# Local attention heads on 64-row tiles: two heads side by side instead of zero halves

## The chip, the cores and the metric

The kernel runs on one core of a Trainium2 chip. The metric is the device time of one execution in microseconds (us), as the median of several runs. The engines are TensorE (PE, with its weight loads as PEld), VectorE (DVE), ScalarE (ACT), GpSimd (POOL) and SyncE (SP), which issues most of the DMAs.

## The reference

Sparse attention (4 batches, 8 heads, 576 positions, head size 64, all fp32) is followed by a top-1 mixture of experts (2304 tokens of width 512, 8 experts, hidden width 1024). Heads 0 to 3 are local: a query sees itself and the 31 positions before it. Heads 4 to 7 are strided: a query sees the earlier positions that leave the same remainder by 32.

```python
mask_local = (rel >= 0) & (rel < stride)                     # heads 0..3, stride = 32
mask_strided = (rel >= 0) & (pos[None] % stride == pos[:, None] % stride)
attn = softmax(where(mask, q @ k.T / 8, -1e9)); x = attn @ v  # then [2304, 512]
expert = argmax(x @ w_gate);  out = gate * relu(x @ w1[expert]) @ w2[expert]
```

## The kernel before, in words

Attention comes first and the experts follow. The attention part is a hand-written software pipeline of 25 steps (line 24, `SEQ`): 16 strided units (`z`) and 9 local units (`l`). A unit passes through five stages: A transposes queries and keys on TensorE and copies them out of PSUM, B makes scores with a mask matmul and narrow matmuls, takes the row maximum and subtracts it (both on DVE), then ACT takes the exponential, C transposes the probabilities, D multiplies with the values and divides by the sum, and E stores the result and transposes it for the gate. In each iteration of the loop that starts at line 928 every engine gets C of unit i, A of i+3, B of i+2, E of i-1 and D of i, in this order. `gating` (line 894) adds gate matmuls (`l_f`), and `drip_out` adds small routing work, most of it on DVE.

A local unit `vv` holds 256 tokens in blocks of 32 queries. Each block needs 64 keys: its own 32 and the 32 before. Two heads (a pair) stand one above the other on the 128 partitions, head 0 on partitions 0 to 63. `K0L` (line 174) is a key tile with a column range for each head, and the half that belongs to the other head is zero; one matmul of 128 rows and 128 columns thus gives the scores of both heads (line 493). `V0L` (line 175) does the same for the values with 130 columns (line 529). The zeros are written by POOL at the start (lines 196 to 207). Each of these fp32 matmuls shows as two instructions in the trace, so the 16 matmuls of a stage show as 32.

`load_l` (line 252) loads the queries and keys of a pair with one DMA each, in runs of 1536 B. `l_r` (line 454) then reorders half of such a tile so that the two heads stand side by side, keys on ACT and queries on DVE, and `l_a` (line 462) transposes the reordered tile on TensorE (line 471) and copies it out: queries on ACT (line 473), keys of head 0 on ACT and of head 1 on DVE (line 477). There are 8 pairs with two halves each, so `l_a` runs 16 times. `load_lv` (line 260) loads the values: a small DMA from POOL (line 266) and, for each head, one DMA from SP of 64 partitions x 17 blocks x 256 B (line 269), which reads nearly each value twice, since a block's row holds the block to its left as well. Values of pairs 4 to 7 reuse the four tiles and so wait for stage D of earlier units.

Loads are put on SP's queue by a planner (`load_more`, line 851) in the order in which they fall due; behind one another stand the strided keys and queries (`load_z`, line 235), strided values (`load_zv`, line 247), `load_l` and `load_lv`. ACT's queue issues the stores of x. Score tiles of both kinds share one PSUM pool, `ps_s`, with two buffers (line 145). The expert part (from line 1089) is dense fp32r matmuls and starts when the first expert is known.

Of the kernel before, what the change touches and what calls it, by code (L numbers as in the profile page):

```python
# [29 lines left out]
RB = 2  # L30
RE = "sv"
ZSTR = "001 3cd23"
ZS = {int(a[0]): a[1:] for a in ZSTR.split()}
TY = 2
# [7 lines left out]
VE = "gg"  # L42
VL = 2
NBS = "-1 0 1 2"
NB = dict(zip(("zq", "zv", "lq", "lv"), map(int, NBS.split())))
ND = 0
RJ = 0
RL = 2
LS = 1
RM = 1  # L50
# [18 lines left out]
def kernel(  # L69
# [68 lines left out]
    with ExitStack() as p1:  # L138
# [6 lines left out]
        ps_s = p1.enter_context(tc.tile_pool(name="ps_s", bufs=2, space=PSUM))  # L145
# [28 lines left out]
        K0L = [cp.tile([128, 2, 608], F32, name=f"k0l{i}") for i in range(4)]  # L174
        V0L = [cp.tile([128, 2, 18, 65], F32, name=f"v0l{i}") for i in range(4)]
# [20 lines left out]
        def zeros_k(i):  # L196
            nc.gpsimd.memset(K0L[i][0:64, 1], 0.0)
            nc.gpsimd.memset(K0L[i][64:128, 0], 0.0)
            for h in range(2):
                nc.gpsimd.memset(K0L[i][64 * h:64 * h + 64, h, 0:32], 0.0)  # L200

        def zeros_v(i):
            nc.gpsimd.memset(V0L[i][0:64, 1], 0.0)
            nc.gpsimd.memset(V0L[i][64:128, 0], 0.0)
            for h in range(2):
                nc.gpsimd.memset(V0L[i][64 * h:64 * h + 64, h, :, 64], 1.0)
                nc.gpsimd.memset(V0L[i][64 * h:64 * h + 32, h, 0, 0:64], 0.0)

        zeros_k(0)
        zeros_k(1)  # L210
# [41 lines left out]
        def load_l(c):  # L252
            b, pair = divmod(c, 2)
            h0 = 2 * pair
            for src, dst, nm in ((k, lk, "lk"), (q, lq, "lq")):
                t = ld.tile([96, 2, 6, 64], F32, tag=nm, name=nm)
                nc.sync.dma_start(out=t, in_=src[b, h0:h0 + 2].rearrange("h (p g) d -> p h g d", g=6))
                dst[c] = t

        def load_lv(c):  # L260
            b, pair = divmod(c, 2)
            h0 = 2 * pair
            vt = V0L[c % 4]
            if c >= ND:
                for h in range(2):
                    nc.gpsimd.dma_start(out=vt[64 * h + 32:64 * h + 64, h, 0, 0:64], in_=v[b, h0 + h, 0:32, :])  # L266

                    src = bass.AP(tensor=v.tensor, offset=v[b, h0 + h, 0:1, 0:1].offset, ap=[[D, 64], [32 * D, 17], [1, D]])
                    nc.sync.dma_start(out=vt[64 * h:64 * h + 64, h, 1:18, 0:64], in_=src)
                return  # L270
            for h in range(2):
                nc.sync.dma_start(out=vt[64 * h + 32:64 * h + 64, h, :, 0:64], in_=v[b, h0 + h].rearrange("(k p) d -> p k d", p=32))

        def copy_lv(c):

            vt = V0L[c % 4]
            for h in range(2):
                {"s": nc.scalar.copy, "v": nc.vector.tensor_copy, "g": nc.gpsimd.tensor_copy}[VE[h]](
                    vt[64 * h:64 * h + 32, h, 1:18, 0:64], vt[64 * h + 32:64 * h + 64, h, 0:17, 0:64])
# [96 lines left out]
        def z_b(u):  # L376
            K0 = K0S[u % 2]
            qt = qts.pop(u)
            s = ps_s.tile([128, 4, 2, 36], F32, tag="s", name="sz")
# [72 lines left out]
        lr = {}  # L452

        def l_r(i):

            c, gi = divmod(i, 2)
            for src, nm in ((lk[c], "k"), (lq[c], "q")):
                t = ld.tile([96, 3, 2, 64], F32, tag="r" + nm, name="r" + nm, bufs=RB)
                {"g": nc.gpsimd.tensor_copy, "v": nc.vector.tensor_copy, "s": nc.scalar.copy}[RE[nm == "q"]](t.rearrange("p g h d -> p h g d"), src[:, :, 3 * gi:3 * gi + 3, :])
                lr[i, nm] = t  # L460

        def l_a(c, gi):
            for nm in "kq":
                src = lr.pop((2 * c + gi, nm))
# [5 lines left out]
                for i in range(3):  # L470
                    nc.tensor.transpose(t[:, i, :], src[:, i].rearrange("p h d -> p (h d)"), ident[:96, :96])
                if nm == "q":
                    nc.scalar.copy(QTL[c % 4].rearrange("d (p g) -> d g p", g=6)[:, 3 * gi:3 * gi + 3, :], t)
                else:
                    for h in range(2):
                        r = slice(64 * h, 64 * h + 64)
                        (nc.vector.tensor_copy if h else nc.scalar.copy)(
                            K0L[c % 4][r, h, 32:32 + S].rearrange("d (p g) -> d g p", g=6)[:, 3 * gi:3 * gi + 3, :],
                            t[r],
                        )  # L480

        MSEL = {0: 0, 2: 4, 4: 2, 6: 4}

        def l_b(vv):
            s = ps_s.tile([128, 2, 2, 128], F32, tag="s", name="sl")
            a = {0: 0, 2: 5, 4: 2, 6: 4}.get(vv, 1)
            nc.tensor.matmul(s, lhsT=identb, rhs=bc(ml[:, a:a + 2], 2, 4), start=True, stop=False, skip_group_check=True)
            for t in range(2):
                for pair in range(2):
                    for c in range(4):  # L490
                        b, blk = divmod(4 * (2 * vv + t) + c, 18)
                        n = (2 * b + pair) % 4
                        nc.tensor.matmul(
                            s[32 * c:32 * c + 32, t, pair],
                            lhsT=QTL[n][:, 32 * blk:32 * blk + 32],
                            rhs=K0L[n][:, :, 32 * blk:32 * blk + 64],
                            start=False, stop=True, skip_group_check=True,
                            tile_position=(0, 32 * c),
                        )
            s8 = s.rearrange("p t a (h k) -> p (t a h) k", h=2)  # L500
            mx = tmp.tile([128, 8], F32, tag="mxl", name="mxl")
            nc.vector.tensor_reduce(mx, s8, axis=AX.X, op=ALU.max)
            p = wk.tile([128, 4, 128], F32, tag="pl", name="pl", bufs=2)
            p8 = p.rearrange("p a (h k) -> p (a h) k", h=2)
            nc.vector.tensor_tensor(p8, s8, bc(mx, 2, 64), op=ALU.subtract)
# [15 lines left out]
        def l_d(vv):  # L521
            pt = PTl.pop(vv)
            o = ps_o.tile([128, 2, 512], F32, tag="o", name="ol")
            for t in range(2):
                for pair in range(2):
                    for c in range(4):
                        b, blk = divmod(4 * (2 * vv + t) + c, 18)
                        n = (2 * b + pair) % 4
                        nc.tensor.matmul(  # L529
                            o[32 * c:32 * c + 32, t, 130 * pair:130 * pair + 130],  # L530
                            lhsT=pt[:, 2 * t + pair, 32 * c:32 * c + 32],
                            rhs=V0L[n][:, :, blk, :],
                            start=True, stop=True,
                            tile_position=(0, 32 * c),
                        )
            ov = o[:, :, 0:260].rearrange("p a (j d) -> p a j d", d=65)
# [4 lines left out]
            nc.vector.tensor_tensor(  # L541
                x.rearrange("p (t a) h d -> p t (a h) d", t=2), ov[:, :, :, 0:64], bc(sm, 3, 64), op=ALU.mult,
            )
# [30 lines left out]
        def l_f(vv):  # L574
            xt = xtl.pop(vv)
            lp = LP[:, 2 * vv:2 * vv + 2]
            if vv == 8:
                z = ps_s.tile([128, 2, E], F32, tag="s", name="LPl")
# [197 lines left out]
        def emit_la(m):  # L776
            while la_done[0] < m:
# [3 lines left out]
                if (i, "k") not in lr:  # L781
                    l_r(i)
                for t in ZS.get(i, ""):
                    (zeros_k if t in "abcd" else zeros_v)(ord(t) - 97 if t in "abcd" else int(t))
# [623 lines left out]
```

## Time and profile before

| | us |
|---|---|
| runs | median 406.17, lowest 404.76, highest 408.29 (3 runs) |
| the profiled execution | 402.96, of which the span from first to last instruction is 401.2 |
| PE busy | 359.9 (90%) |
| PEld busy | 321.6 (80%) |
| DVE busy | 244.5 (61%) |
| ACT busy | 185.5 (46%) |
| POOL busy | 97.5 (24%) |
| TensorE's mean granted clock | 0.952 |

A busy share is an average over the attention part, up to about 151 us, and the expert part behind it. An instruction's row gives its engine, source line, output <- inputs, shape, count and time; what stands in brackets is the idle time of the engine just before it and what ended that. SPq, ACTq and POOLq are the queues on which DMAs are issued. A granted clock of 1.00 is 2.4 GHz and 0.50 is 1.2 GHz.

### The profile page before, as it was taken

To read this page: it belongs to the slowest core of one execution; us is meant where nothing else is said; L and a number is where in the kernel's file an instruction comes from. 1 tells how busy PE (TensorE), PEld (TensorE's weight loads), DVE (VectorE), ACT (ScalarE), POOL (GpSimd) and SP (SyncE) were. 2 spreads that over 40 slices of the span, in tenths; PEclk is the share of its full clock that TensorE was granted. 3 is DMA by queue.
4 is the path that set the end of the run, shared out by engine and by line. 5 is a ranking of instruction groups with operands and counts; after the bars stand their busy time and mean duration, and the time that the engine had idled before them with its cause. 6 is when DMAs were issued, how large, how long until landed. Compare 5 with 4: busy or idle time off the path is not lost. (4 is left out here: it accounts for less than half of the span.)

```text
span 401.2 us, 9649 instructions
## 1 busy us (share of the span) xinstructions
PE 359.9 (90%) x3843; PEld 321.6 (80%) x3844; DVE 244.5 (61%) x528; ACT 185.5 (46%) x341; POOL 97.5 (24%) x158
## 2 busy tenths in 40 slices
PE   7688987959888986899999999999999999999980
PEld 3476766848766773898999999999999999989960
DVE  8686772863457887845565475466575666666620
ACT  6466672653556422435424453444445444546510
POOL 8950100010000003307124213414325033113110
PEclk9999996995589999999999999999999999999996
DMA  6889559869312825979666357437556386575000
GB/s 144 201 173 166 163 135 202 168 154 198 96 32 57 164 86 192 214 99 351 205 211 230 108 153 239 158 131 248 168 194 230 107 265 203 182 225 178 3 29 26
DMA packets 73576, 65.07 MB, mean 162 GB/s; under 512 B 34013, under 2 KB 60637, under 8 KB 73522
## 3 DMA queue, kind: packets, MB, share of 16 engines
q1 hardware_dynamic: 61874, 49.84, 47.8%
q0 software_dynamic: 4400, 9.80, 9.0%
q10 hardware_dynamic: 7248, 4.72, 4.3%
q8 instruction: 32, 0.52, 0.6%
q14 instruction: 22, 0.18, 0.2%
HBM read 54.90 MB, written 9.60 MB: 161 GB/s over the span
## 5 line engine op out<-in xcount | busy, mean ns | idle before, releaser
L1142 PE MATMUL ph<-xh,w1h 128*128 128x280 f32 (+5 forms) x252 | 78.7, 312 | 0.0
L1144 PE MATMUL ph<-xh,w1l 128*128 128x280 f32 (+5 forms) x252 | 75.4, 299 | 0.0
L1143 PE MATMUL ph<-xl,w1h 128*128 128x280 f32 (+5 forms) x252 | 75.3, 299 | 0.0
L1159 ACT ACTIVATE hh<-ph 128x280 fp32r<-128x280 f32 (+5 forms) x64 | 26.8, 419 | 86.5 <-PE ph L1144 84.7
L1143 PE MATMUL y<-hl,w2h 128*128 128x280 f32 (+4 forms) x192 | 58.7, 306 | 0.8 <-DVE hl L1160 0.8
L1144 PE MATMUL y<-hh,w2l 128*128 128x280 f32 (+4 forms) x192 | 58.6, 305 | 0.0
L1142 PE MATMUL y<-hh,w2h 128*128 128x280 f32 (+4 forms) x192 | 58.4, 304 | 0.0
L1160 DVE SCALAR_TENSOR_TENSOR hl<-ph,hh 128x280 fp32r<-128x280 f32 (+5 forms) x64 | 29.7, 464 | 40.4 <-ACT hh L1159 39.6
L1188 POOL DMA_INDIRECT out_dram<-yo,routing x22 | 21.9, 994 | 128.5 <-DVE yo L1213 99.1
L1122 DVE TENSOR_TENSOR w1l<-w1r,w1h 128x1024 fp32r<-128x1024 f32 x31 | 38.0, 1227 | 17.3 <-ACT w1h L1121 16.3
L1142 PEld LDWEIGHTS ph<-xh,w1h 128*128 128x128 f32 x252 | 47.6, 189 | 0.5
L1143 PEld LDWEIGHTS ph<-xl,w1h 128*128 128x128 f32 x252 | 47.7, 189 | 0.3
L1144 PEld LDWEIGHTS ph<-xh,w1l 128*128 128x128 f32 x252 | 47.5, 189 | 0.0
L1122 DVE TENSOR_TENSOR w2l<-w2r,w2h 128x1024 fp32r<-128x1024 f32 x32 | 39.1, 1221 | 2.5 <-ACT w2h L1121 1.8
L1143 PEld LDWEIGHTS y<-hl,w2h 128*128 128x128 f32 x192 | 36.1, 188 | 1.2 <-DVE hl L1160 1.1
L1142 PEld LDWEIGHTS y<-hh,w2h 128*128 128x128 f32 x192 | 36.2, 188 | 0.0
L1121 ACT CAST w2h<-w2r 128x1024 fp32r<-128x1024 f32 x32 | 33.6, 1049 | 5.5 <-PE y L1143 4.3
L1144 PEld LDWEIGHTS y<-hh,w2l 128*128 128x128 f32 x192 | 36.1, 188 | 0.0
L1121 ACT CAST w1h<-w1r 128x1024 fp32r<-128x1024 f32 x31 | 32.2, 1039 | 3.6 <-DMA w1r<-in_moe_w_dram 3.6
L1225 POOL DMA_INDIRECT gt<-g_dram,routing x22 | 23.9, 1087 | 16.3 <-DMA g_dram<-GA 9.9
L131 POOL DMA_INDIRECT xg<-x_dram,routing x19 | 20.6, 1085 | 23.4 <-PE px L1132 12.5
L266 POOL DMA_DIRECT2D v0l<-in_v_dram x16 | 8.2, 521 | 57.7 <-PE ol L529 57.7
(221 smaller groups left out, 692.1 us busy)
## 6 DMA issues: line engine op xcount, KB each, us to landing
w1r<-in_moe_w_dram SPq DMA_DIRECT2D x32, 512.0 KB
w2r<-in_moe_w_dram SPq DMA_DIRECT2D x32, 512.0 KB
v0l<-in_v_dram SPq DMA_DIRECT2D x16, 272.0 KB
zk<-in_k_dram SPq DMA_DIRECT2D x16, 144.0 KB
zq<-in_q_dram SPq DMA_DIRECT2D x16, 144.0 KB
v0s<-in_v_dram SPq DMA_DIRECT2D x32, 72.0 KB
lk<-in_k_dram SPq DMA_DIRECT2D x8, 288.0 KB
lq<-in_q_dram SPq DMA_DIRECT2D x8, 288.0 KB
```

The source lines that it names most:

```text
L131: nc.gpsimd.indirect_dma_start(out=t[:r], out_offset=None, in_=x_dram[:, :], in_offset=bass.IndirectOffsetOnAxis(ap=idx[:r], axis=0),)
L266: nc.gpsimd.dma_start(out=vt[64 * h + 32:64 * h + 64, h, 0, 0:64], in_=v[b, h0 + h, 0:32, :])
L1121: nc.scalar.copy(hi, t)
L1122: nc.vector.tensor_tensor(lo, t, hi.bitcast(F32), op=ALU.subtract)
L1142: nc.tensor.matmul(o, lhsT=wh, rhs=xh, start=first, stop=False)
L1143: nc.tensor.matmul(o, lhsT=wh, rhs=xl, start=False, stop=False)
L1144: nc.tensor.matmul(o, lhsT=wl, rhs=xh, start=False, stop=last)
L1159: nc.scalar.activation(hh, o, AF.Relu)
L1160: nc.vector.scalar_tensor_tensor(hl, o, 0.0, hh.bitcast(F32), op0=ALU.max, op1=ALU.subtract)
L1188: s = nc.gpsimd.indirect_dma_start(out=out[:, :], out_offset=bass.IndirectOffsetOnAxis(ap=idx, axis=0), in_=o, in_offset=None, bounds_chec ...
L1225: nc.gpsimd.indirect_dma_start(out=t[:r], out_offset=None, in_=g_dram[:, :], in_offset=bass.IndirectOffsetOnAxis(ap=idx_r(i)(j)[:r], axis=0),)
```

## The change

Each head of a pair now has its own matmul on 64 rows, at row 0 or 64 of the array, with 64 columns (scores) or 65 (values). A stage has 32 such matmuls in place of 16. The zero halves and POOL's memsets for them go. Scores and outputs of the two heads stand in two PSUM banks, so a score tile takes two banks, and `ps_s` has one buffer in place of two. Queries and keys come from DRAM with the heads side by side, two DMAs for a tile in runs of 256 B, and `l_r` goes. Keys are copied out of PSUM in one piece on DVE, queries on ACT, with positions outermost. Values are loaded once for each head, on partitions 32 to 63 of the half (32 partitions x 18 blocks x 256 B), by SP; POOL then copies 17 blocks to partitions 0 to 31, shifted by one block, and its small DMAs go. Local masks take two matmuls of 256 columns in place of one of 512.

```diff
-        ps_s = p1.enter_context(tc.tile_pool(name="ps_s", bufs=2, space=PSUM))
+        ps_s = p1.enter_context(tc.tile_pool(name="ps_s", bufs=1, space=PSUM))
...
-        K0L = [cp.tile([128, 2, 608], F32, name=f"k0l{i}") for i in range(4)]
-        V0L = [cp.tile([128, 2, 18, 65], F32, name=f"v0l{i}") for i in range(4)]
+        KTL = [cp.tile([128, S], F32, name=f"ktl{i}") for i in range(4)]
+        VLL = [cp.tile([128, 18, 65], F32, name=f"vll{i}") for i in range(4)]
...
-        zeros_k(0)
-        zeros_k(1)
+        for i in range(4):
+            nc.gpsimd.memset(VLL[i][:, :, 64], 1.0)
+            for h in range(2):
+                nc.gpsimd.memset(VLL[i][64 * h:64 * h + 32, 0, 0:64], 0.0)
...
-                t = ld.tile([96, 2, 6, 64], F32, tag=nm, name=nm)
-                nc.sync.dma_start(out=t, in_=src[b, h0:h0 + 2].rearrange("h (p g) d -> p h g d", g=6))
+                t = ld.tile([96, 6, 2, 64], F32, tag=nm, name=nm)
+                for h in range(2):
+                    nc.sync.dma_start(out=t[:, :, h, :], in_=src[b, h0 + h].rearrange("(p g) d -> p g d", g=6))
...
-                    nc.gpsimd.dma_start(out=vt[64 * h + 32:64 * h + 64, h, 0, 0:64], in_=v[b, h0 + h, 0:32, :])
-                    src = bass.AP(tensor=v.tensor, offset=..., ap=[[D, 64], [32 * D, 17], [1, D]])
-                    nc.sync.dma_start(out=vt[64 * h:64 * h + 64, h, 1:18, 0:64], in_=src)
+                nc.sync.dma_start(out=vt[64 * h + 32:64 * h + 64, :, 0:64], in_=v[b, h0 + h].rearrange("(k p) d -> p k d", p=32))
+            for h in range(2):
+                nc.gpsimd.tensor_copy(vt[64 * h:64 * h + 32, 1:18, 0:64], vt[64 * h + 32:64 * h + 64, 0:17, 0:64])
...
-                src = lr.pop((2 * c + gi, nm))
...
-                    nc.tensor.transpose(t[:, i, :], src[:, i].rearrange("p h d -> p (h d)"), ident[:96, :96])
-                if nm == "q":
-                    nc.scalar.copy(QTL[c % 4].rearrange("d (p g) -> d g p", g=6)[:, 3 * gi:3 * gi + 3, :], t)
-                else:
-                    for h in range(2):
-                        (nc.vector.tensor_copy if h else nc.scalar.copy)(K0L[c % 4][64 * h:64 * h + 64, h, ...], t[64 * h:64 * h + 64])
+                    nc.tensor.transpose(t[:, i, :], src[:, 3 * gi + i].rearrange("p h d -> p (h d)"), ident[:96, :96])
+                dst = QTL if nm == "q" else KTL
+                {"s": nc.scalar.copy, "v": nc.vector.tensor_copy}[LE[nm == "q"]](dst[c % 4].rearrange("d (p g) -> d p g", g=6)[:, :, 3 * gi:3 * gi + 3], t.rearrange("d g p -> d p g"))
...
-                        nc.tensor.matmul(s[32 * c:32 * c + 32, t, pair], lhsT=QTL[n][:, 32 * blk:32 * blk + 32],
-                            rhs=K0L[n][:, :, 32 * blk:32 * blk + 64], ..., tile_position=(0, 32 * c))
+                        for h in range(2):
+                            nc.tensor.matmul(s[32 * c:32 * c + 32, h, o + k0:o + 64],
+                                lhsT=QTL[n][64 * h:64 * h + 64, 32 * blk:32 * blk + 32],
+                                rhs=KTL[n][64 * h:64 * h + 64, 32 * blk - 32 + k0:32 * blk + 32], ..., tile_position=(64 * h, 32 * c))
...
-                            lhsT=pt[:, 2 * t + pair, 32 * c:32 * c + 32], rhs=V0L[n][:, :, blk, :], ..., tile_position=(0, 32 * c))
+                            for h in range(2): ...
+                                lhsT=pt[64 * h:64 * h + 64, i, 32 * c:32 * c + 32], rhs=VLL[n][64 * h:64 * h + 64, blk, :], ..., tile_position=(64 * h, 32 * c))
```

(Long lines of the diff are cut with "..."; `LE = "vs"` puts keys on DVE and queries on ACT.)

## Rows read from the trace of the kernel before

**Rows 1.** Busy time of the engines in stretches of the span. Columns: stretch and its length, then busy us and instructions of PE, PEld, DVE, ACT, POOL, then granted TensorE clock, busy share of the DMA engines, GB/s.

```profile
0.00:89.70 89.70, 71.97 (x1061) 54.48 (x1062) 61.77 (x165) 51.33 (x115) 28.06 (x92) 0.96 0.78 167
89.70:113.60 23.90, 22.64 (x254) 17.75 (x258) 9.50 (x21) 9.34 (x21) 0.00 (x0) 0.50 0.73 134
113.60:128.00 14.40, 11.25 (x190) 8.76 (x184) 9.90 (x20) 10.40 (x22) 0.00 (x0) 1.00 0.11 33
128.00:151.00 23.00, 21.33 (x722) 17.20 (x715) 19.29 (x84) 8.45 (x16) 0.00 (x0) 1.00 0.57 122
```

**Rows 2.** What PE waited for in the first 151 us: us in total, times, longest.

```profile
PE tl L471 <- ACT rk L459: 6.5, 4, 2.6
PE tq L364 <- DMA zk<-in_k_dram: 3.7, 2, 2.7
```

**Rows 3.** Such waits one by one, from the timeline of PE. Columns: start, duration, engine, line, operation; in brackets the wait before it.

```profile
61.44 0.44 PE L364 MATMUL tq<-ident,zk 72*128 72x72 f32 x4 [2.67 <-DMA zk<-in_k_dram]
87.61 0.45 PE L364 MATMUL tq<-ident,zk 72*128 72x72 f32 x4 [1.06 <-DMA zk<-in_k_dram]
89.87 0.71 PE L364 MATMUL tq<-ident,zq 72*128 72x72 f32 x4 [1.82 <-DMA zq<-in_q_dram]
104.66 0.74 PE L471 MATMUL tl<-ident,rk 96*128 96x96 f32 x3 [1.09 <-ACT rk L459]
118.81 0.47 PE L471 MATMUL tl<-ident,rk 96*128 96x96 f32 x3 [1.07 <-ACT rk L459]
125.15 0.47 PE L471 MATMUL tl<-ident,rk 96*128 96x96 f32 x3 [1.79 <-ACT rk L459]
```

**Rows 4.** SP's queue in order of time: start of the first issue, time until the end of the last one of the group, line, DMA, count.

```profile
48.03 9.12 SPq L247 DMA_DIRECT2D v0s<-in_v_dram  x8
...
57.25 1.46 SPq L235 DMA_DIRECT2D zk<-in_k_dram  x2
...
62.57 0.32 SPq L257 DMA_DIRECT2D lk<-in_k_dram  x1
...
64.05 9.20 SPq L269 DMA_DIRECT2D v0l<-in_v_dram  x4
...
83.98 0.91 SPq L235 DMA_DIRECT2D zk<-in_k_dram  x2
...
127.69 3.63 SPq L269 DMA_DIRECT2D v0l<-in_v_dram  x4
```

**Rows 5.** What SP's queue waited for before it could issue a value load: us in total, times, longest.

```profile
SPq L269 <- DMA x_dram<-xz: 5.2, 1, 5.2
```

**Rows 6.** Narrow matmuls on the timeline of PE: local scores at full clock, local outputs at half clock and at full clock (unit 6), the first and the last group of the 64 gate matmuls of one `l_f` at full clock, strided scores at half and at full clock; last, from the view of line 529, the shortest, median and longest of its matmuls in ns.

```profile
74.30 1.08 PE L493 MATMUL sl<-k0l,qtl 128*32 128x128 f32 x32
...
66.20 1.96 PE L529 MATMUL ol<-v0l,ptl 128*32 128x130 f32 x32
...
138.75 1.10 PE L529 MATMUL ol<-v0l,ptl 128*32 128x130 f32 x32
...
72.37 0.31 PE L589 MATMUL R__103<-wg,xtl 128*32 128x8 f32 x16
...
72.81 0.37 PE L589 MATMUL R__103<-wg,xts 128*32 128x8 f32 x14
...
64.23 1.18 PE L383 MATMUL sz<-k0s,qt 128*36 128x72 f32 x16
...
70.13 0.70 PE L383 MATMUL sz<-k0s,qt 128*36 128x72 f32 x16
...
L529 PE MATMUL ol<-v0l,ptl x288: 271/273/425, 44.6 to 146.6; 128*32 128x130 f32 x144
```

**Rows 7.** Groups of instructions up to 135 us, shapes kept apart: busy us, mean ns of one; then idle time before them and what ended it.

```profile
L477 DVE COPY k0l<-tl 64x288 f32<-64x288 f32 x16 | 10.9, 681 | 13.1 <-ACT k0l L477 13.1
L477 ACT COPY k0l<-tl 64x288 f32<-64x288 f32 x16 | 10.7, 669 | 3.2 <-PE tl L471 3.2
L459 ACT COPY rk<-lk 96x384 f32<-96x384 f32 x16 | 8.5, 529 | 2.8 <-DMA lk<-in_k_dram 2.8
L459 DVE COPY rq<-lq 96x384 f32<-96x384 f32 x16 | 6.9, 430 | 3.9 <-DMA lq<-in_q_dram 3.6
```

**Rows 8.** Packets of the hardware queue that SP feeds, from the DMA views of three stretches, in this order: 30 to 40 us (most of them 256 B), 50 to 57 us (most of them 256 B), 60 to 66 us (most of them 1536 or 2048 B). Columns: packets, MB, time that they took as a share of 16 engines in the stretch.

```profile
q1 hardware_dynamic: 4933, 1.34, 100.1%
...
q1 hardware_dynamic: 1930, 0.62, 35.6%
...
q1 hardware_dynamic: 756, 1.26, 85.3%
```

**Rows 9.** POOL and DVE: first two lines of the timeline, then two groups of POOL's instructions (busy us, mean ns | idle before).

```profile
22.45 1.30 DVE L459 COPY rq<-lq 96x384 f32<-96x384 f32 x1
22.47 1.07 POOL L204 MEMSET v0l<- 64x1170 f32 x1
...
L203 POOL MEMSET v0l<- 64x1170 f32 x4 | 4.3, 1066 | 0.2
...
masks.py:199 POOL TENSOR_SCALAR_AFFINE_SELECT ident<-ident 128x128 f32<-128x128 f32 x1 | 0.3, 291 | 0.1
```

**Rows 10.** The timeline where PE starts the mask matmul of one score tile before DVE has read the previous one.

```profile
34.05 0.38 PE L487 MATMUL sl<-ml,identb 128*128 128x512 bf16 x1
...
34.35 0.46 DVE L391 TENSOR_TENSOR pz<-sz,mx 100x288 f32<-100x288 f32 x1
```

More of the change, by code (lines that the diff above doesn't have):

```diff
@@ L262, in load_lv @@
             h0 = 2 * pair
[L263 to L270 removed]
+            vt = VLL[c % 4]
             for h in range(2):
[L272 to L276 removed]
+                nc.sync.dma_start(out=vt[64 * h + 32:64 * h + 64, :, 0:64], in_=v[b, h0 + h].rearrange("(k p) d -> p k d", p=32))
             for h in range(2):
[L278 to L279 removed]
+                nc.gpsimd.tensor_copy(vt[64 * h:64 * h + 32, 1:18, 0:64], vt[64 * h + 32:64 * h + 64, 0:17, 0:64])
         load_z(0)
@@ L450, with l_a @@
         Pl, PTl, Xl, suml, xtl = {}, {}, {}, {}, {}
-        lr = {}
-        def l_r(i):
-            c, gi = divmod(i, 2)
+        def l_a(c, gi):
             for src, nm in ((lk[c], "k"), (lq[c], "q")):
[L458 to L463, printed above, removed]
-                src = lr.pop((2 * c + gi, nm))
                 t = ps_t.tile([128, 3, 96], F32, tag="t", name="tl")
@@ L528, in l_d @@
                         n = (2 * b + pair) % 4
[L529 to L536, printed above, removed]
+                        i = 2 * t + pair
+                        for h in range(2):
+                            nc.tensor.matmul(
+                                o[32 * c:32 * c + 32, h, 65 * i:65 * i + 65],
+                                lhsT=pt[64 * h:64 * h + 64, i, 32 * c:32 * c + 32],
+                                rhs=VLL[n][64 * h:64 * h + 64, blk, :],
+                                start=True, stop=True,
+                                tile_position=(64 * h, 32 * c),
+                            )
+            ov = o[:, :, 0:260].rearrange("p h (i d) -> p h i d", d=65)
             sm = tmp.tile([128, 2, 4], F32, tag="sml", name="sml")
@@ L780, in emit_la @@
                 load_to("lq", i // 2)
[L781 to L784, printed above, removed]
-                if RM == 2 and 0 < i < 15 and nload["lq"] > (i + 1) // 2:
-                    l_r(i + 1)
                 l_a(i // 2, i % 2)
                 la_done[0] += 1
-                if i < 15 and (i + 1, "k") not in lr and nload["lq"] > (i + 1) // 2 and (i % 2 == 0 or RM):
-                    l_r(i + 1)
         def l_need(vv):
@@ L840, in need_ @@
             return at["l", 18 * (c // 2) // 8]
-        copied = [0]
-        def copy_to(m):
-            while copied[0] < m:
-                load_to("lv", copied[0])
-                if copied[0] < ND:
-                    copy_lv(copied[0])
-                copied[0] += 1
         def load_more(i):
-            for c in range(copied[0], min(nload["lv"], 8)):
-                if need("lv", c) <= i + VL:
-                    copy_to(c + 1)
             while True:
@@ L940 @@
             drip_out(1)
-            for j in range(la_done[0], min(la_done[0] + RJ, 16)):
-                if (j, "k") not in lr and nload["lq"] > j // 2 and lstep.get(j // 2, -9) + RL <= i:
-                    l_r(j)
-            n0 = nload["lq"]
             load_more(i)
-            for c in range(n0, nload["lq"]):
-                lstep[c] = i
             if i == 0:
```

64 lines of the change are left out of this document (18 added, 46 removed).

## Prediction

> **What bounds the kernel now.** I first cut the span into stretches [rows 1]. The attention part ends at about 151 us; the rest is dense expert work that the diff does not touch. So whatever the change is worth lies ahead of 151 us, and behind it the end only moves along. In that part PE is busy in 71.97 of the first 89.70 us and in 22.64 of the next 23.90 us. Those 23.90 us ran at a granted clock of 0.50, which is 1.2 GHz, and just before the clock fell PE had stood almost idle for over 3 us. From 128 to 151 us DVE is busy in 19.29 of 23.00 us and PE in 21.33, so there both count.
>
> Then I asked what PE waited for [rows 2]: reordered keys on ACT, 6.5 us, and strided keys from DRAM, 3.7 us; strided queries come on top. One by one [rows 3], the DRAM waits stand in two places, before 63.4 us and from 86.6 to 89.87 us, and the late ACT waits at 104.66, 118.81 and 125.15 us. SP's queue says why the loads are late [rows 4]: the first pair of strided keys is issued at 57.25 us behind a group of value loads that took 9.12 us, the second at 83.98 us behind value loads that began at 64.05 us. Part of that is not work: a value load stood 5.2 us until a store of x had landed [rows 5].
>
> This shapes the whole sum. What PE saves ahead of a DRAM wait is lost in that wait, unless the load itself comes sooner. Only savings behind 89.87 us reach the end.
>
> **The change part by part.** The sum is made against the profiled execution (402.96 us with its span of 401.2), which lies 3.2 us under the median of 406.17; differences are then put on the median.
>
> *Narrow matmuls.* 32 instructions of 128 or 130 columns take 1.08 to 1.10 us at full clock and 1.96 us at half [rows 6]. Without the last one's own duration, 0.27 us or 0.42 [rows 6], that is 0.81 us, 26 ns from start to start, or 1.54 us. Now there are 64 of half the columns. The lower bound is half the columns with twice as many tiles side by side: 0.40 us. The upper bound is that each new instruction takes the place of an old one: 64 x 26 ns = 1.64 us. The row nearest to it is the gate's, also 64 instructions with 32-column weights but with 8 columns: 72.37 to 73.18 us in all; with 0.18 us off for the last one (an estimate: 16 of them together take 0.31) that is 0.63 us or 10 ns each [rows 6]. I take 0.63 us at full clock, and at half clock, scaled as strided scores are (1.18 against 0.70), 1.06 us. A group thus gains 0.18 us at full clock and about 0.5 us at half.
>
> Behind 89.87 us stand two score groups at half clock and, at full clock up to 128 us, one score and two output groups: 2 x 0.5 + 3 x 0.18 = 1.5 us. In the last stretch the chain runs through PE only near its end: 0.2 us more. The six groups ahead of 89.87 us gain some 1.4 us, which I give to the DRAM waits.
>
> The Trainium skill, "TensorE: Matmul & The Clock Gate", section "Wait — 56ns, not 53.3ns?", states that start-to-start of matmuls never falls below about 25 ns however few the columns. By that a group would take 64 x 25 = 1.6 us, an estimate from that page, and this change would cost PE where my sum has a gain. The gate's rows do not agree: 10 ns on 32-column tiles; a rival below carries the case.
>
> *Reorder copies.* 16 ACT copies of 529 ns and 16 DVE copies of 430 ns go [rows 7]. What is on the path is the wait behind them: 1.09 + 1.07 + 1.79 = 3.95 us [rows 3]. The rest of the 6.5 us, 2.6 at the first pair, stays: there the copy itself waited for the load. I count the 3.95 whole. What is late next is the copies out of PSUM, and these shrink too: ACT's 16 key copies of 669 ns go, while DVE's of 681 ns stay, now on 128 partitions [rows 7]. No row shows the new order of elements. I take their time as unchanged, since the elements per partition are; bounds are the 430 ns of a reorder copy and twice 681. Even at twice, DVE, busy in 9.90 of 14.40 us ahead of 128 us [rows 1], has the room.
>
> *Loads.* Per pair, queries and keys go from 2 x 192 pieces of 1536 B to 4 x 576 of 256 B, and values from 2 x 1088 pieces of 256 B (plus a small one by POOL) to 2 x 576. A 256 B packet took 100.1% of 160 us / 4933 = 32 ns where the engines were full and 35.6% of 112 us / 1930 = 21 ns where not; a large one 85.3% of 96 us / 756 = 108 ns [rows 8]. Over all pairs and 16 engines: queries and keys +3 to +17 us, values -11 to -17 us, in sum -7.5 to 0. At worst the engines gain nothing, so this term is zero. SP's own time counts: a load of 192 pieces takes 0.32 us to issue, one of 288 pieces 1.1 with waits (9.12 / 8), one of 1088 pieces 0.9 in the quiet group at 127.69 us [rows 4]. At 0.7 us each, four query and key loads cost 2 us more per pair, and two value loads about 0.5 less, more where the engines hold the queue up. Ahead of 57.25 us this adds about 1 us, partly taken up by the standing wait for a store; ahead of 83.98 us extra and saved issues about cancel. I take +0.5 us in all, bounds -1.3 and +4.
>
> *Values copied by POOL.* 16 copies of 32 x 1088 elements; no row shows one. By memset (1066 ns for 1170 elements) it is 1.0 us at least; by the only POOL operation here that reads and writes SBUF (291 ns for 128) 2.5 us at most [rows 9]. I take the middle, 1.7. The first three batches have time. The last cannot start before stage D of unit 4; its loads went out at 127.69 us [rows 4] and unit 6 needs them at 138.75 [rows 6], 11 us later. First landing after about 4 us, then 4 x 1.7: 10.8 us. It just fits; at 2.5 us unit 6 is 3 us late. DVE, busy there in 19.29 of 23 us, may be held up too: its reorder copy took 1.30 us against a mean of 430 ns when a POOL memset ran beside it [rows 9]. If POOL's copies stopped DVE for their whole time, that is 6.9 us; if not, 0. I take +1.5 us in all.
>
> The Trainium skill, "SBUF — State Buffer", section "Who interferes with whom", states that a DVE instruction with two SBUF inputs and a GpSimd instruction that reads SBUF exclude each other for their whole length. By it the routing work, full of such instructions, would pay most of the 6.9 us. The row shows only a copy beside a memset, and no run here shows the other pair.
>
> *One score buffer.* A mask matmul now waits for the subtract of the step before. Once that was not done yet: 34.05 us against 34.35 + 0.46 [rows 10], so 0.8 us there, ahead of a DRAM wait; near 136 us it is about 0.6 us, half of it hidden behind DVE. I take +0.3.
>
> *Memsets.* POOL's (4.3 us for one of their lines [rows 9]) are written for tiles that are used much later, and other work of PE covers them: 0.
>
> Sum: -1.5 - 0.2 - 3.95 + 0.5 + 1.5 + 0.3 = -3.35 us. The profile would give about 399.6 us, the median **402.8**.
>
> **The rivals.**
> (a) The clock holds. If fewer value packets bring the strided loads forward and PE's second gap closes, the 23.90 us at 0.50 shorten. The same score group takes 1.18 us at half and 0.70 at full clock [rows 6], so they would take about 14.2 where PE is the limit: 9 us less, 393 to 394 us. For it: the gap came just before the fall. Against: the queue is paced by stores as well.
> (b) Row tiles do not run side by side, so that the change does not do what it says on PE: 8 narrow column slots as before, no gain. Then -3.35 + 1.7, so 404.5.
> (c) POOL's last batch and the hold-up of DVE cost 6 us rather than 1.5: 407. For it: the 1.30 us; against: no row shows DVE's two-input instructions held up.
> (d) SP's queue becomes the bound, **slower**: more DMAs at 0.7 us each, and one more standing wait like the 5.2 us ahead of each pair of strided loads. PE's two gaps grow by about 5 us each, and everything behind runs later; less the 4 us kept: 411 to 412. It decides from the point where the loads now at 57.25 and 83.98 us go out more than 3 us later relative to PE. For it: SP already waits for landings; against: less value traffic.
> (e) Each narrow matmul holds its slot for 26 ns, as the page has it: 0.83 us more for each of 18 groups and twice that for three of them is 17 us; some 5 vanish in DRAM waits: 402.8 + 1.7 + 12, so 416. Against: the gate's 10 ns.
>
> **How the numbers follow.** Chances: forecast 0.36, (a) 0.16, (b) 0.13, (c) 0.10, (d) 0.16, (e) 0.09. The forecast's own range is 399 to 406. About 1%, 4 us, is what a measurement here tells from no change: faster is below 402.1, slower above 410.2. Faster: all of (a) and over half of the forecast's range, 0.38; slower: (d), (e), 0.26; within: 0.36. To hold 8 in 10 the range takes in (a) to (d) and leaves out (e) and the far ends: 393 to 413.
>
> **What would show it.** Narrow groups: 64 instructions in about 0.9 us with their tail at full clock. Waits of PE for ACT at the local transposes gone behind 100 us. POOL copies of 1.7 us; the last of them ending before unit 6's outputs start. Strided loads at about the same distance from PE, two DRAM gaps, and a half-clock stretch of some 20 us. I am wrong if the clock's stretches move by more than 5 us, since that outweighs every other term; if PE's rows show 1.6 us for a group; or if DVE's small instructions between 128 and 140 us are several times as long as now.

## The result, and the profile after

The change made the kernel slower by 1.4%: 406.95 us median of 20 runs (403.71 to 415.68) against 402.72 of 20 runs of the kernel before (397.37 to 410.16); the ratio is 1.0139, 95% interval 1.0108 to 1.0170. (A median is over all runs, a ratio over those within 1.5% of the fastest of their kernel, so the two can differ, and where too few such runs are left no ratio is given.) The forecast was a gain of 3.35 us. The execution profiled with that result took 414.5 us, 7.5 over its median; so the rows below are of a second profile of the changed kernel, run e0, of 404.82 us with a span of 403.1. That is 1.9 us more than the profiled execution of before.

Stretches of the span of e0 (columns as in [rows 1]):

```profile
14.40:24.60 10.20, 9.27 (x57) 6.94 (x58) 2.29 (x5) 1.87 (x5) 0.00 (x0) 0.50 0.91 165
...
41.80:52.00 10.20, 8.97 (x73) 7.23 (x73) 3.40 (x9) 2.68 (x7) 4.35 (x4) 0.50 0.69 142
...
69.10:79.30 10.20, 8.76 (x183) 7.36 (x184) 2.96 (x8) 2.23 (x6) 0.00 (x0) 0.50 0.76 167
...
93.00:103.20 10.20, 7.74 (x111) 5.97 (x111) 3.71 (x9) 2.96 (x8) 0.00 (x0) 0.50 0.75 171
...
130.00:153.00 23.00, 17.21 (x765) 13.46 (x759) 17.49 (x72) 7.12 (x14) 3.36 (x4) 1.00 0.20 63
```

Four stretches of 10.2 us at a clock of 0.50, which is 1.2 GHz, stand where [rows 1] had one of 23.9 us (and a short one ahead of it). In the last 23 us PE is busy only 17.21 us, against 21.33 of 23.00 in the last stretch of before.

What PE waited for in e0 up to 155 us (columns as in [rows 2]):

```profile
PE tl L432 <- DMA lk<-in_k_dram: 5.0, 2, 2.8
PE tq L336 <- DMA zq<-in_q_dram: 4.5, 2, 2.4
PE tq L336 <- DMA zk<-in_k_dram: 2.1, 2, 1.8
...
PE sl L449 <- issue: 1.6, 2, 1.3
...
PE tl L432 <- DMA lq<-in_q_dram: 1.4, 1, 1.4
PE R__103 L544 <- issue: 1.4, 1, 1.4
PE ol L486 <- issue: 1.3, 2, 1.1
...
PE sl L440 <- DVE pl L460: 0.6, 1, 0.6
PE LPl L544 <- issue: 0.4, 1, 0.4
```

The waits for reordered keys of [rows 2] are gone. New are waits for local keys and queries from DRAM and "issue", pauses for which the profile names no releaser: 4.7 us in four lines, none of which before has. Both on the timeline of PE, with a narrow group at half and one at full clock between them:

```profile
41.14 0.44 PE L432 MATMUL tl<-ident,lk 96*128 96x96 f32 x3 [2.21 <-DMA lk<-in_k_dram]
43.03 0.71 PE L432 MATMUL tl<-ident,lq 96*128 96x96 f32 x3 [1.45 <-DMA lq<-in_q_dram]
...
73.40 1.20 PE L486 MATMUL ol<-vll,ptl 64*32 64x65 f32 x64
...
82.39 0.86 PE L449 MATMUL sl<-ktl,qtl 64*32 64x64 f32 x64
...
128.72 0.32 PE L449 MATMUL sl<-ktl,qtl 64*32 64x32 f32 x8 [1.35 <-issue]
...
140.95 0.27 PE L544 MATMUL R__103<-wg,xtl 128*32 128x8 f32 x11 [1.44 <-issue]
...
144.79 0.31 PE L486 MATMUL ol<-vll,ptl 64*32 64x65 f32 x5 [1.07 <-issue]
```

At 41 us PE stands for 2.21 and 1.45 us, and the clock falls at 41.8. The narrow groups take 1.20 us at half and 0.86 us at full clock. The last three rows are the middle of groups: 56 of 64 score matmuls done, 1.35 us of nothing, then the other 8.

SP's queue in e0 (columns as in [rows 4]):

```profile
27.07 1.16 SPq L217 DMA_DIRECT2D zk<-in_k_dram  x2
34.99 0.72 SPq L217 DMA_DIRECT2D zq<-in_q_dram  x2
35.81 1.29 SPq L240 DMA_DIRECT2D lk<-in_k_dram  x2
37.20 1.76 SPq L240 DMA_DIRECT2D lq<-in_q_dram  x2
```

And what it waited for up to 60 us, first line:

```profile
SPq L217 <- DMA x_dram<-xz: 9.9, 2, 6.7
```

The third pair's local keys go out at 35.81 us; before, at 26.39. Strided queries stand ahead of them, and these could not go until 34.99: SP stood on a store of x.

Copies of DVE, ACT and POOL in e0 (busy us, mean ns | idle before):

```profile
L251 POOL COPY vll<-vll 32x1088 f32<-32x1088 f32 x13 | 14.2, 1089 | 109.7 <-DMA vll<-in_v_dram 109.3
...
L434 ACT COPY qtl<-tl 128x288 f32<-128x288 f32 x16 | 7.6, 478 | 19.1 <-PE tl L432 19.1
...
L434 DVE COPY ktl<-tl 128x288 f32<-128x288 f32 x16 | 7.4, 462 | 10.6 <-PE tl L432 10.3
```

ACT's copies of the queries in the kernel before, which [rows 7] does not show:

```profile
L473 ACT COPY qtl<-tl 128x288 f32<-128x288 f32 x16 | 11.2, 701 | 1.0 <-PE tl L471 0.9
```

DVE and POOL on the timeline near the last batch of value copies:

```profile
131.93 0.49 DVE L594 TENSOR_TENSOR r_ge<-POS,th 128x24 f32<-128x24 f32 x1
...
132.54 1.02 DVE L599 TENSOR_TENSOR r_a<-r_ge 128x20 f32<-128x20 f32 x1
...
129.00 4.53 POOL L251 COPY vll<-vll 32x1088 f32<-32x1088 f32 x4 [16.41 <-DMA vll<-in_v_dram]
```

### The profile page after: what moved, and what is told of

The parts are those of the page before. It is cut to its first block, busy times and chain, and to the rows that moved or that the text cites. A ratio compares the mean times of both kernels' runs of the same rounds, so it can differ in the third digit from the quotient of the medians.

```text
span 412.7 us, 10734 instructions
## 1 busy us (share of the span) xinstructions
PE 370.7 (90%) x4428; PEld 330.7 (80%) x4429; DVE 233.2 (57%) x512; ACT 167.6 (41%) x309; POOL 91.3 (22%) x130
## 5 line engine op out<-in xcount | busy, mean ns | idle before, releaser
L251 POOL COPY vll<-vll 32x1088 f32<-32x1088 f32 x16 | 17.4, 1089 | 119.7 <-DMA vll<-in_v_dram 119.1
```

Of the source, the lines that this page charges most:

```text
L251: nc.gpsimd.tensor_copy(vt[64 * h:64 * h + 32, 1:18, 0:64], vt[64 * h + 32:64 * h + 64, 0:17, 0:64])
```

## The experiments

The median of each run stands beside one of before from the same chip. Letters name theories: Q and Q2 SP's queue, S the load buffer, P the small pieces, C and E the clock, V a loss behind 130 us, F the supply of instructions to PE.

### The loads: e0 to e3

**e0** is the changed kernel as it is.

> The changed kernel as it is, for a second profile beside its own times. The profiled run that came with the result took 414.5 us with some 65 us at half clock ahead of the experts, 7.5 us over that kernel's median. Theory Q (late key and query loads starve PE, and the clock falls for it): 405 to 409 us, the third pair's keys still waited for near 41 us, and 45 to 70 us at half clock against 30.7 before. Rival V (the loss lies behind 130 us, in the POOL copies, the single score buffer and PE's instruction supply): same time, but half clock near 31 us and the experts later by a loss between 130 and 165 us.

**e1**, both heads by one DMA:

```diff
-for h in range(2):
-    nc.sync.dma_start(out=t[:, :, h, :], in_=src[b, h0 + h].rearrange("(p g) d -> p g d", g=6))
+nc.sync.dma_start(out=t, in_=src[b, h0:h0 + 2].rearrange("h (p g) d -> p g h d", g=6))
```

> The changed kernel, but both heads of a key or query tile come by one DMA of 1152 pieces of 256 B instead of two of 576: the same pieces, 16 DMAs fewer, so as many as before the change. Theory Q (number of DMAs: each new one waits until the one eight places before it has landed, x stores among them): 401 to 404 us, the wait at 41 us under 1 us or gone, half clock down by 15 us or more. Rival P (the small pieces themselves are slow): no change, 405 to 409 us, the wait stays above 2 us. Rival S (the load buffer is freed late, by the transposes): no change either.

**e2**:

```diff
-t = ld.tile([96, 6, 2, 64], F32, tag=nm, name=nm)
+t = ld.tile([96, 6, 2, 64], F32, tag=nm, name=nm, bufs=3)
```

> The changed kernel with three buffers instead of two for local keys and for local queries, so that the third pair's loads wait for no transpose. Rival S (late release of the buffer, which the reorder copies used to give early): the wait for keys at 41 us is gone and the fall of the clock behind it too, 403 to 405 us. Theory Q: the queue is held by landings, not by the buffer, so the loads go out less than 1.5 us sooner and the time stays at 405 to 409 us.

**e3**, the loads of before, with `l_r` and its copies put back as they were:

```diff
-t = ld.tile([96, 6, 2, 64], F32, tag=nm, name=nm)
+t = ld.tile([96, 2, 6, 64], F32, tag=nm, name=nm)
+nc.sync.dma_start(out=t, in_=src[b, h0:h0 + 2].rearrange("h (p g) d -> p h g d", g=6))
```

> The changed kernel with the local keys and queries loaded and reordered as before (one DMA of 1536 B pieces each, copies by ACT and DVE); 64-row tiles, the POOL copies of the values and the single score buffer stay. Theories Q, S and P: 400 to 403 us, half clock near 31 us; if the 3.95 us of waits for reordered keys return, toward the upper end. Rival V: 405 to 409 us, as the changed kernel.

Against 401.57 us (9 runs) of before: e0 407.15 (ratio 1.0293, 1.0084 to 1.0502), e1 404.94 (1.0284, 1.0137 to 1.0431), e2 403.09 (1.0196, 1.0109 to 1.0283), e3 407.09 (1.0290, 1.0176 to 1.0404). In e1 and e2 the strided queries still go out at 35.69 and 34.93 us, the keys behind them, and PE still waits for them, 2.4 to 3.1 us near 42 us: neither the number of DMAs nor the buffer holds them up, though e2's time lies in the range that S gave. In e3 the keys go out at 24.59 us and the loss is as large, as rival V had it. Q, S and P as first put fall; something that e3 kept costs as much.

### Stores off SP's lanes, and the first gap: e4, e5, e9

In the trace of e0 each load of SP and each store of ACT ends on one of eight completion semaphores ("lanes"), taken in turn, and waits for the landing of that lane's last user. A store that ACT issued at 32.28 us is the last user for the strided queries, which SP reached at 28.2 us and issued at 34.99.

**e4** (both places; 25 stores):

```diff
-nc.scalar.dma_start(
+nc.gpsimd.dma_start(
     out=x_dram[...
```

> The changed kernel with the 25 stores of x issued by POOL instead of ACT, so that they leave the round of completion semaphores that SP's loads share with them. Theory Q2 (three buffers and fewer DMAs did not bring the third pair's keys forward, since their queue stands 5 to 8 us on an x store that comes just before them in that round): SP's waits for x stores ahead of 60 us are gone, the keys go out near 28 us instead of 35.8, PE's wait at 41 us is under 1 us and the clock does not fall at 41.8; 397 to 403 us if POOL's issue costs nothing. Rival E (the early falls of the clock come one from another and not from the gaps): the fall at 41.8 stays. Rival V (all of it lies behind 130 us): 405 to 409 us.

**e5**:

```diff
-XFS = "12 6 6 6"
+XFS = "28 6 6 6"
```

> The changed kernel with 28 instead of 12 filling matmuls ahead of the first local transposes, so that PE, which stood idle from 12.5 to 15.2 us, is at work until the first keys land. Theory C (the clock falls where PE has just stood idle): no fall at 14.5 us, the one at 41.8 stays; half clock down by about 10 us, and since 17 us of work there ran at half clock partly beside waits, 1 to 4 us less: 403 to 406. Rival E (the falls come one from another, 27.3 us apart): the later ones move or go as well. Rival V: 405 to 409 us.

**e9**, e4 with

```diff
-name="xz", bufs=2)   name="xl", bufs=2)
+name="xz", bufs=4)   name="xl", bufs=3)
```

> The changed kernel with stores by POOL, four buffers instead of two for the strided x tiles and three instead of two for the local ones, so that POOL's value copies (4.5 us a batch, 37.5 to 42 us in the run with stores by POOL) do not keep DVE and then PE from going on. PE stood 5.6 us there and the clock fell behind it. Theory (the store waits behind the copies on POOL's queue, the x buffer behind the store): the 5.6 us are gone, 385 to 390 us. Rival (PE would only wait for the next load there): 390 to 393.

e4: 391.45 us against 400.18 (13 runs), faster than any theory had it; its four runs go from 387.64 to 399.51. SP's queue in e4:

```profile
26.10 0.92 SPq L217 DMA_DIRECT2D zk<-in_k_dram  x2
27.12 0.73 SPq L217 DMA_DIRECT2D zq<-in_q_dram  x2
27.95 1.29 SPq L240 DMA_DIRECT2D lk<-in_k_dram  x2
```

And the longest wait of PE in e4:

```profile
PE tx L405 <- DVE xz L395: 5.6, 1, 5.6
```

The keys go out at 27.95 us and the wait at 41 us is gone: the cause of the late loads is Q2's. The 5.6 us are POOL's own queue, where stores stand behind 4.53 us of value copies; with more x buffers they go, and e9 takes 388.56 us against 398.60 (7 runs; ratio 0.9710, 0.9571 to 0.9849). e5: 405.42 us in 10 runs (398.98 to 412.90; ratio 1.0060, 1.0000 to 1.0120), by its median as slow as the changed kernel and by its ratio nearer to before. Its clock fell at 17.1 us instead of 14.4 and again at 41.0 and 68.3, so filling that gap spared no fall, and C is not shown by it.

### Parts taken out of the changed kernel: e6, e7, e16

**e6**, values of the block to the left loaded a second time:

```diff
-nc.gpsimd.tensor_copy(vt[64 * h:64 * h + 32, 1:18, 0:64], vt[64 * h + 32:64 * h + 64, 0:17, 0:64])
+nc.sync.dma_start(out=vt[64 * h:64 * h + 64, 1:18, 0:64], in_=src)
```

> The changed kernel with the values of the block to the left loaded a second time from DRAM, as before, and not copied by POOL; everything else as changed. Theory of the prediction's rival (c) (POOL's copies hold up the end): 3 to 5 us faster than the changed kernel, 402 to 404. Theories Q2 and C: the added traffic delays loads, so no gain: 405 to 410 us.

**e7**, the gate on 128 columns:

```diff
-nc.tensor.matmul(lp[32 * c:32 * c + 32, t], lhsT=l, rhs=wg[:, d], ..., tile_position=(0, 32 * c))
+nc.tensor.matmul(lp[:, t], lhsT=l, rhs=wg[:, d], ...)
```

> The changed kernel with the gate's matmuls on all 128 columns of PE, 8 a unit instead of 32 on 32-column tiles: 216 matmuls and as many weight loads fewer, all between 125 and 160 us. Theory F (in this stretch PE uses up instructions faster than 16 KB blocks of them are brought in, which is where it pauses in the midst of a group with nothing to wait for, 3 to 5 us in sum): the pauses shrink below 1.5 us and the experts start 2 to 4 us sooner for the same clock, 402 to 406 us. Rival (those pauses have another cause, a late operand that the trace doesn't name): they stay, 405 to 409 us or more, as 8 wide matmuls are no faster than 32 narrow ones.

**e16**, `l_b`, `l_d`, K0L, V0L and two score buffers as before; loads and POOL's copies as changed:

```diff
-lhsT=QTL[n][64 * h:64 * h + 64, 32 * blk:32 * blk + 32], ..., tile_position=(64 * h, 32 * c)
+lhsT=QTL[n][:, 32 * blk:32 * blk + 32], rhs=K0L[n][:, :, 32 * blk:32 * blk + 64], ..., tile_position=(0, 32 * c)
```

> The changed kernel with the 64-row tiles taken out: 128-row matmuls with zero halves and two score buffers, as before; new key and query loads, no reorder copies, values of the block to the left copied by POOL, stores by ACT. Theory F (the 1,154 added instructions on PE are the loss, by pauses and by the clock behind them): 390 to 397 us, pauses under 3 us, half clock near 30 us. Rival (the loads and the order of SP's lanes are the loss): 403 to 408 us, as the changed kernel.

e6: 415.77 us against 400.18, in four runs from 406.34 to 419.70. None of them reaches the 402 to 404 of rival (c), so POOL's copies are not the loss; what they gain is not measured, since the runs spread too far for a ratio. e7: 425.48 us, far over both ranges; its pauses are all gone, as F expected, but 96 instructions of its wide gate matmuls took 19.3 us of PE, at least half of them at 1.2 GHz, so its time says nothing. e16: 399.63 us against 400.22 (7 runs; ratio 0.9987, 0.9914 to 1.0060). Without the 64-row tiles, and with two score buffers again, the loss is gone, and so is every pause; the interval lies clear of the 1.0108 to 1.0170 of the changed kernel. It is slower than the 390 to 397 expected: SP still stood up to 7.7 us on a store, and PE waited 4.2 us for strided and 3.1 for local keys.

### Parts put alone on the kernel before: e8, e10 to e15, e17

**e8** and **e15**: before, with the edit of e4.

> The kernel before the change, with its 25 stores of x issued by POOL, as the changed kernel had them when it took 391.5 us. It tells what the change itself is worth when no load stands behind a store. If the sum of the prediction was right for everything but the queue (-3.35 us): 393 to 397 us here, 2 to 5 us more than the changed kernel with the same edit. Rival G (the gain belongs to the stores alone and the change is worth nothing): 390 to 392. Rival H (before, SP's queue hardly mattered, 40 us at half clock is its own): 398 to 402.

> The kernel before with stores by POOL once more, to be compared with the two edits above on one chip: 386 to 390 us.

**e14** and **e12** (with the edit of e4): the changed `l_b` and `l_d` on the tiles of before, one score buffer.

```diff
-lhsT=QTL[n][:, 32 * blk:32 * blk + 32], rhs=K0L[n][:, :, 32 * blk:32 * blk + 64], ..., tile_position=(0, 32 * c)
+lhsT=QTL[n][64 * h:64 * h + 64, 32 * blk:32 * blk + 32],
+rhs=K0L[n][64 * h:64 * h + 64, h, 32 * blk:32 * blk + 64], ..., tile_position=(64 * h, 32 * c)
```

> The kernel before with the 64-row tiles and the single score buffer alone, stores by ACT as they were. Theory F alone: 1 to 4 us over the kernel before, 400 to 404. Theory Q2 (the order of loads and stores on SP's lanes moves with every edit): it can be further off than that, up to 410, if stores come to stand ahead of key loads. Prediction's terms: 397 to 398.5.

> The kernel before with stores by POOL and with the 64-row tiles and the single score buffer alone; loads, reorder copies, zero halves in memory and values stay as before. Theory F (the added instructions cost pauses): PE's pauses with nothing to wait for grow from 2.9 us to 5 us or more ahead of the experts, and the time is 388 to 393 us, slower than without the edit. Prediction's terms (-1.7 for the matmuls, +0.3 for the score buffer): 385.5 to 387.

**e10**: before, with each gate matmul twice, the second on weights `wz` of zero.

```diff
 nc.tensor.matmul(lp[...], lhsT=l, rhs=wg[:, d], ..., tile_position=(0, 32 * c))
+nc.tensor.matmul(lp[...], lhsT=l, rhs=wz[:, d], ..., tile_position=(0, 32 * c))
```

> The kernel before the change with each of the gate's 32-column matmuls issued a second time on zero weights: 288 matmuls and as many weight loads more, about half of what the change adds, all of them where the pauses of the changed kernel lie. Theory F (PE runs out of instructions): pauses of PE in the midst of groups with nothing to wait for appear, 1 to 3 us in sum ahead of the experts, where before has none, and the time grows by 3 us of matmuls and by them: 404 to 408 us. Rival (they belong to the 64-row tiles): no such pause, 402 to 405.

**e13**: e8 with the changed `load_l` and no reorder copies, so also with the new order in the copies out of PSUM. **e11**: e3 with the edit of e4. **e17**: e16 with the edit of e4 and three xz buffers.

> The kernel before with stores by POOL and with the new key and query loads alone (two DMAs of 576 pieces each, no reorder copies); 128-row matmuls with zero halves, two score buffers and doubled value loads stay. Prediction's terms (-3.95 for the waits, +0.5 for the loads) and theory F (nothing added on PE): 383 to 386 us, PE's waits for reordered keys gone, pauses as without the edit near 2.9 us. Rival (the loads take from the queue what the copies gave): 387 to 390.

> The changed kernel with stores by POOL and with local keys and queries loaded and reordered as before: against the 391.5 us with the new loads it prices the second part of the change with SP's queue free. Prediction's term (copies gone -3.95, loads +0.5): 394 to 396 us. Rival (the loads come late again, only less, and eat it up): 390 to 392.5 us.

> The same with the 25 stores by POOL and three buffers instead of two for the strided x tiles. Theories F and Q2 add up: 374 to 383 us, faster than the kernel before, the changed one and both of them with stores by POOL. If the store lanes are all there is: 386 to 390.

```
run   us       before   ratio, 95% interval            run   us       before   ratio, 95% interval
e8    387.69   398.60   0.9673, 0.9558 to 0.9788       e12   400.36   399.90   none; runs 389.21 to 402.69
e15   385.84   399.90   0.9607, 0.9530 to 0.9684       e13   390.00   399.90   none; runs 380.31 to 394.88
e14   415.21   399.90   1.0344, 1.0250 to 1.0437       e11   392.61   398.60   0.9759, 0.9622 to 0.9895
e10   424.75   398.60   1.0628, 1.0492 to 1.0764       e17   389.08   400.22   0.9719, 0.9649 to 0.9788
```

The 64-row tiles with the single score buffer alone cost 3.4% (e14), 13.8 us, more than any theory had it. Not all of it need be theirs: in the profile of e14, of its slowest run (424.76 us), SP stood up to 10.2 us on one store, where its longest such wait in before is 5.2 [rows 5]:

```profile
SPq L247 <- DMA x_dram<-xz: 11.1, 2, 10.2
```

With stores by POOL their price stays open: the four runs of e12 go from 389.21 to 402.69 us, those of e15 from 383.98 to 393.21. And the whole change costs nothing there that can be told from noise: e9 (the changed kernel, with more x buffers), e17 (the 64-row tiles taken out) and e8 (the kernel before) stand at 0.9710, 0.9719 and 0.9673, each well inside the intervals of the others. So the tiles cost where stores share the lanes with loads; that they cost by themselves is not shown.

PE's pauses up to 180 us in e14, in e12, in e15 and in e10 (us in total, times, longest):

```profile
PE R__103 L592 <- issue: 5.7, 3, 2.5
...
PE sl L497 <- issue: 3.6, 2, 2.5
...
PE ol L534 <- issue: 1.1, 2, 0.6
```

```profile
PE R__103 L592 <- issue: 4.9, 3, 1.9
PE sl L497 <- issue: 3.0, 1, 3.0
```

```profile
PE R__103 L589 <- issue: 2.5, 2, 1.9
```

```profile
PE R__103 L591 <- issue: 8.6, 4, 3.5
...
PE sl L495 <- issue: 1.3, 1, 1.3
```

Before has none in its profile; 288 gate matmuls more (576 instructions in the trace, 10 ns from start to start) give it 9.9 us of them (1 to 3 expected), and the narrow tiles 7.9 to 10.4. Instructions reach PE by a DMA queue of their own (`q8 instruction` in the DMA view), 16 KB at a time: 37 such blocks in e0, 32 in before. Worked out from the traces, the longest pause of each of six kernels and the block that was on its way:

```
kernel  pause of PE (us)      block of instructions (us)   pause ends after landing
e0      139.51 to 140.95      138.29 to 139.45             1.50
e9      110.78 to 112.80      110.26 to 111.24             1.56
e10      73.98 to  77.47       74.70 to  76.10             1.37
e12     127.04 to 130.00      126.93 to 128.33             1.67
e14     147.92 to 150.41      147.52 to 148.92             1.49
e15      65.57 to  67.45       65.10 to  66.08             1.37
```

Of 80 such pauses of 0.25 us or more between 20 and 170 us in all traces, 79 end 1.1 to 1.7 us after a block has landed. PE had run out of instructions, as theory F has it. Their sum is 4.3 to 10.4 us in every kernel with 64-row tiles but e7, and 0 to 3.8 in those without but e10. What stands behind one, in e12 (columns as in [rows 1]):

```profile
126.20:129.60 3.40, 0.83 (x41) 0.48 (x39) 2.64 (x10) 0.57 (x2) 0.72 (x1) 1.00 1.18 183
129.60:136.40 6.80, 6.40 (x124) 4.92 (x123) 2.44 (x5) 1.71 (x3) 1.30 (x2) 0.50 0.03 8
```

Around the pause from 127.04 to 130.00 PE was busy 0.83 of 3.40 us; then 6.8 us ran at 1.2 GHz. That is the common picture: of the 90 falls of the clock between 12 and 165 us in all traces, 85 stand close beside a wait or pause of PE of 1 us or more, 16 of them beside a pause without a releaser. There are 184 such waits and pauses, so not each of them brings a fall. In e0 none of its four long stretches at 1.2 GHz begins at such a pause; they begin beside waits for loads and, the last, for ACT.

e8 lies below all three of its ranges, e15 just below its own, e10 far over both of its ranges. e13 decides nothing: waits for reordered keys gone, pauses 3.8 us, but runs from 380.31 to 394.88 us. e11 is 6.0 us faster than its before and e4 8.7, a difference that the interval of e11 takes in, so the price of the new loads stays open. e17 missed its 374 to 383; almost without pauses, it had a new wait of PE:

```profile
PE ol L521 <- POOL v0l L279: 6.1, 3, 2.5
```

Outputs waited for POOL's value copies, which shared POOL's queue with the stores. The lowest medians are those of the kernel before with its stores by POOL, 385.84 and 387.69 us; e9 and e17 cannot be told from them, and all four are faster than both kernels compared here.

**The clock over all runs.** Each run lists span and mean granted clock; 2 x (1 - clock) x span is its time at 1.2 GHz. Over the runs that enter the ratios, the mean is 36.3 us for 31 runs of before and 51.1 for 19 of the changed kernel. Two straight lines of one slope through them give 0.23 us of time for each us at half clock, and 4.2 us between the kernels at the same clock. Of the 7.6 us between their means (398.7 and 406.3), 14.8 x 0.23 = 3.4 go with the clock. This is a fit and no experiment: through all 43 and 25 runs the slope is 0.33, with 5.1 of 7.8 us.

## Why the prediction was wrong

Wrong in sign, and by one step above all. That 406.95 us lies between 393 and 413 is no merit of the sum: its base, 406.17 us, was a median of three runs, 3.5 us above that of 20, and (d), a loss, had set the upper end.

- **Narrow matmuls, -1.7 us: the step that failed.** The group's time was right: 0.86 us, of which the last one's own are 0.22, leaves 10 ns from start to start; rivals (b) and (e) fall. The Trainium skill, "TensorE: Matmul & The Clock Gate", section "Wait — 56ns, not 53.3ns?", states a floor of about 25 ns from start to start. These groups do not keep to it, with 10. But the term counted matmuls by their time and not by their number. PE's matmul instructions go from 3843 to 4428, and as many weight loads come with them; a group is 128 instructions in 0.64 us, and the next block comes too late: 4.7 us of pauses in e0, none in before. In place of -1.7 and +0.3 for the score buffer (one wait of 0.6 us in e0) the runs show +6 within the changed kernel (1.0139 of before with the narrow tiles, 0.9987 without, e16) and +13.8 alone (e14). How much of that is the pauses, how much the clock and how much the order of loads and stores is not shown apart: with stores by POOL e9 has pauses too (2.2, 2.0 and 1.9 us are its largest sums), and is no slower than e17, which is almost without them but has the 6.1 us wait for POOL. The score buffer and the split mask were never tried without the tiles. The Trainium skill, "Runtime: NRT & Kernel Launch", section "Instruction fetch mechanics", states that instructions come in blocks of 256 and that the cost of crossing into the next one is mostly hidden. Blocks of 16 KB the traces show; hidden it is not here.
- **The clock.** The text named stretches that move by over 5 us as what would make it wrong. They moved: 44.4 us at half in the first 165 us of e0 against 30.7, and 14.8 us on the mean of the runs above. The sum had no term for it; a gap pays twice where the clock falls behind it.
- **Reorder copies, loads and values: -3.95 + 0.5 + 1.5 = -1.95 us.** Together they came to -0.6 (e16, whose interval takes in -3.4 to +2.4), so this part may stand, but not by its terms. The waits for reordered keys went, and the copies out of PSUM shrank where they were to stay: DVE's of the keys from 681 ns [rows 7] to 462, ACT's of the queries from 701 to 478.
- **Loads.** Their issue took 0.65 to 0.88 us each (0.7 taken). What was missed is where the standing wait for a store [rows 5] would go: ahead of the third pair's local keys, 9.4 us late, 3.7 us of PE. Rival (d) had the mechanism and looked at the strided pairs. Freed of it the changed kernel goes from 1.4% over before to 2.9% under (e9), but the kernel before gains as much or more, 3.3% and 3.9% (e8, e15). So the shared lanes are no cost of the change alone: they were there before, and the sum took them as given.
- **Values by POOL.** A copy takes 1.09 us, near the lower bound of 1.0; the batch ends at 133.53 us. Beside it r_a, with both inputs in SBUF, took 1.02 us and ended at 133.56, and r_ge, also with both in SBUF, 0.49, where the same instructions of before take 0.17 and 0.18. That is 1.2 us in this batch, not 6.9 (4 x 1.7 is 6.8). The Trainium skill, "SBUF — State Buffer", section "Who interferes with whom", has a DVE instruction with two SBUF inputs and a GpSimd instruction that reads SBUF exclude each other. The trace agrees for these two. Rival (c) falls, since e6, without the copies, was not faster.

Rival (a) fell with the clock. Not settled: why e10 costs 26 us, more than its pauses, its matmuls and its 17.6 us more at half clock explain; what POOL's copies gain; and why parts do not add up. Each edit also deals the eight lanes anew, so a part put alone carries its own order of loads and stores.

## What to carry to other kernels

Price small instructions by their number too: where a group runs at 10 ns each, look for pauses without a releaser and hold them against the instruction queue in the DMA view. Before a load is called cheap, see which store stands ahead of it on its completion lane; stores on a queue of their own were worth 3.3 to 3.9% here (e8, e15), and with them the whole change nothing that can be told from noise. And a gap of a few us can cost again in the clock behind it.

## What the runs showed of the hardware that was not expected

PE goes on 1.1 to 1.7 us after a block of instructions has landed, not at once. And of the gate matmuls in fp32 those with 128 columns took 122 ns for an instruction at full clock (16 in 1.95 us, e7) and 220 at half (48 in 10.57), where those on 32 columns side by side take 10 at full clock. An instruction of VectorE with both inputs in SBUF took up to six times as long beside a copy of GpSimd (r_a, 1.02 us against 0.17) and ended as the copy did, while a reduce with one input, r_lo, took 0.17 as before.
